# Polysketch attention and a wave MLP on one core: zero matmuls in TensorE's early gaps, and the work of GpSimd given to VectorE

## Chip, core and metric

The kernel runs on one core of one Trainium2 chip. The metric is device time in microseconds (us): before the change 283.65 us, the median of three runs (283.55 to 283.65). The profiled execution has a span of 282.6 us from its first instruction to its last, at a mean granted TensorE clock of 0.962. Engines: PE is TensorE (PEld its weight loads), DVE VectorE, ACT ScalarE, POOL GpSimd, SP the engine that issues the DMAs.

## What is computed

Two blocks in a row. First an attention with a sketched kernel: with `phi(x)` the 64 products of two 8-wide projections of x,

```python
a = einsum('rd,bhsd->bhsr', S1, x); b = einsum('rd,bhsd->bhsr', S2, x)
phi = einsum('bhsi,bhsj->bhsij', a, b).reshape(..., 64)
kv, z = einsum('bhsf,bhsd->bhfd', phi(k), v), phi(k).sum(axis=2)
attn = einsum(phi(q), kv) / (einsum(phi(q), z) + 1e-6)     # 4 batches, 4 heads, 1088 tokens, 32
```

Then, with x the attention output as 4 batches of 1088 x 128:

```python
theta = x @ w_theta
y = einsum('ts,bsd->btd', w_tok_r, x * cos(theta)) + einsum('ts,bsd->btd', w_tok_i, x * sin(theta))
u = x + y
out = u + maximum(u @ w_ch, 0)
```

The weights come as 64-bit floats and are unpacked on the chip. The denominator of the attention can come close to zero, so the sums behind it are kept in several slices of lower precision that are exact in themselves; this is most of the small work of the first third.

## The kernel before

The 1088 tokens are nine chunks of 128 (the last is half full), handled in three groups of three chunks. A batch goes through these stages.

- **Key sums** (`key_sums`). ACT squares k for a scale; DVE rounds k to a bf16 slice, subtracts it, rounds the remainder to a second slice (1152 columns each). PE multiplies the slices with themselves (18 bf16 matmuls of 128x256 and 128x128). What is left, the "rest of k", is another subtraction: for batch 0 on DVE in three pieces of 384, for batches 1 to 3 on POOL in three pieces of 384; then a 1152-column scalar_tensor_tensor on DVE and nine fp32 matmuls.
- **Key features** (`kfeatures`). PE transposes k, ACT copies it, PE multiplies by the block matrix `sbk` (128x64 for each chunk), ACT copies the 192 columns of a group from PSUM into `ks`, and POOL forms the outer products in pieces of 256 columns: 3 pieces x 3 groups x 4 batches = 36. PE then sums them with v. The pieces wait for `gate`, which a POOL copy writes after the chain of batch 0.
- **Chain** (`chain`): some 25 small DVE operations and a few small matmuls which turn the key sums into the last columns of the query matrices `mv` and `mf`. Batch 0 has a chain of its own; batches 1, 2 and 3 share one.
- **Query** (`query_slices`, `levels`, `outputs_x`): q is transposed, scaled, sliced, multiplied by `mv` and `mf` (the "levels", 36 matmuls for each batch), the denominator is worked out on DVE in `lv`, and outer products of `lv` are formed, on DVE for batch 0 (three operations of 768 columns) and on POOL for batches 1 to 3 (27 pieces of 256). They are transposed, multiplied with kv, and then theta, sine and cosine give `z`, the moving side of the mixing (`zs<-ps,g`, 768 columns, once for each full group).
- **Mixing** (`mix_row`): 17 rows of token weights (128 x 1088, fp32) for each batch, three matmuls each: 204 matmuls, the bulk of PE's work. A row must be unpacked first (`weight`): three activations on ACT (L610, L612, L614) and two operations on DVE (a shift of 1088 columns, L360, and an integer add, shown as CUSTOM_DVE_ANT_0 of 2176 uint16).
- **Output** (`mix_out`): add, multiply by w_ch, relu, add, DMA out.

The order of all this is not the order of the text. Every operation is registered with an engine, a cost and its buffers (`op`, `vop`); `Layout.run` works a due time back from the end, adds a shift for the operation's stage from the table `SHIFT`, and `forward` lays out one order for each engine by due time, cost and free buffers. Then `issue` writes the instructions in that order. On the chip every engine takes its instructions strictly in that order. So costs, shifts and the choice of engine all move the order; the hardware's own timing does not.

Line numbers in the profile are those of the kernel before. Most operations go through helpers: L356 is every tensor_tensor, L360 every tensor_scalar, L363 every scalar_tensor_tensor, L372 every plain matmul, so groups are told apart by their tiles.

Of the kernel before, what the change touches and what calls it, by code (L numbers as in the profile page):

```python
# [22 lines left out]
P = 128  # L23
# [11 lines left out]
    "blocks_k": -115.0, "blocks_m": -165.9, "blocks_t": 172.5, "chain0": -493.9, "chain1": -25.2, "den0": -154.1,  # L35
    "den1": -0.6, "den2": 550.3, "den3": 155.9, "first": -13.6, "gate": 68.2, "grid0": -47.2, "grid1": -361.7,
    "grid2": -154.8, "grid3": 138.2, "kT0": -616.5, "kT1": -15.8, "kT2": -106.5, "kT3": 114.8, "keys0": 58.1,
    "keys1": -64.3, "keys2": -6.4, "keys3": 9.8, "kf0": -371.9, "kf1": 82.0, "kf2": -122.3, "kf3": -269.6,
    "kv0": 177.9, "kv1": -3.1, "kv2": -165.7, "kv3": -145.7, "kvb0": -73.2, "kvb1": 78.1, "levels0": 27.7,
    "levels1": -326.9, "levels2": 9.3, "levels3": 197.7, "loadk0": -211.2, "loadk1": 67.3, "loadk2": -116.1,  # L40
    "loadk3": 80.6, "loadq0": -176.1, "loadq1": -113.3, "loadq2": 36.5, "loadq3": 71.0, "loadv0": -5.3,
    "loadv1": -52.2, "loadv2": -248.7, "loadv3": -299.6, "mix0_0": 129.2, "mix1_0": 202.6, "mix1_1": 115.4,
    "mix1_2": 151.5, "mix2_0": 347.7, "mix2_1": 356.4, "mix2_2": 310.8, "mix3_0": -119.0, "mix3_1": -118.6,
    "mix3_2": 366.5, "num0_0": -225.0, "num0_1": -212.0, "num0_2": -155.2, "num1_0": -203.1, "num1_1": -151.6,
    "num1_2": -192.6, "num2_0": -37.1, "num2_1": -88.4, "num2_2": 110.9, "num3_0": 55.3, "num3_1": 19.1,
    "num3_2": -106.3, "out0_0": -36.1, "out0_1": 126.0, "out0_2": 20.0, "out1_0": 347.1, "out1_1": 95.9,
    "out1_2": 143.3, "out2_0": 709.5, "out2_1": 7.1, "out2_2": -127.5, "out3_0": 347.1, "out3_1": -81.0,
    "out3_2": 475.1, "q00": 131.5, "q01": 143.4, "q02": 329.5, "q03": 362.9, "qT0": -50.6, "qT1": -265.7,
    "qT2": -56.8, "qT3": 76.7, "qscale0": 126.6, "qscale1": -94.7, "qscale2": -43.4, "qscale3": 44.4, "rest0": -58.6,
    "rest1": -254.4, "rest2": -245.4, "rest3": -265.7, "row0": -150.0, "row1": 39.7, "row10": 44.3, "row11": 49.1,  # L50
    "row12": 50.4, "row13": 49.7, "row14": 50.7, "row15": 56.2, "row16": -107.5, "row2": 27.1, "row3": 5.8,
    "row4": -56.8, "row5": 44.6, "row6": 40.1, "row7": -5.9, "row8": -184.9, "row9": 39.3, "scaled": -96.4,
    "sliced": 94.2, "small": -110.5, "square2": -101.4, "sums0": 317.9, "sums1": 343.8, "sums2": 425.5,
    "sums3": 183.2, "theta0_0": -278.2, "theta0_1": -308.1, "theta0_2": 44.1, "theta1_0": -213.8, "theta1_1": -58.7,
    "theta1_2": -139.2, "theta2_0": 183.5, "theta2_1": 199.8, "theta2_2": 168.6, "theta3_0": -54.6,
    "theta3_1": 142.0, "theta3_2": 139.8, "w2": -16.1,
}
LOAD_LEAD = 60.0
RAW_LEAD = 30.0
CHAINS = ((0,), (1, 2, 3))  # L60
QPOOL = (False, True, True, True)
# [19 lines left out]
class Layout:  # L81


    START = {"P": 1.3, "V": 0.8, "A": 0.7, "G": 1.3, "S": 0.5}
    ISSUE = 0.4
# [71 lines left out]
    def forward(self):  # L157
# [21 lines left out]
        def place(o):  # L179
            t = 0.0  # L180
            need = {}
            for b in o.bufs:
                if b.slot is None and b.cls is not None:
                    need.setdefault(b.cls, []).append(b)
            for c, bs in need.items():
                av = sorted(s[0] for s in slots[c] if s[1] is None)
                last = max((b.due, b.ops[0]) for b in bs)
                before = bisect.bisect_left(pending[c], last, key=lambda x: x[:2]) - len(bs) + 1
                if len(av) < len(bs) + min(max(before, 0), self.RESERVE[c]):
                    return None  # L190
                t = max(t, av[len(bs) - 1])
            return t

        while done < len(ops):
            pick = None
            for e in "PVAGS":
                cand = []
                for o in ready[e]:
                    t = max(free[e], o.ready, o.due - o.lead)
                    p = place(o)  # L200
                    if p is None:
                        continue
                    t = max(t, p)
                    if o.lk:
                        a, z, n = port["V" if e == "G" else "G"]
                        if a <= t < z:
                            t = z if n == 1 else min(z, t + 0.25)
                    cand.append((t, o))
                if not cand:
                    continue  # L210
                first = min(c[0] for c in cand)
                t, o = min((c for c in cand if c[0] <= first + self.SLACK[e]), key=lambda c: (c[1].rank, c[1].i))
                if pick is None or t < pick[0]:
                    pick = (t, o)
            if pick is None:
                raise RuntimeError("no room: " + str([(o.eng, round(o.due), [b.name for b in o.bufs]) for e in "PVAGS"
                                                      for o in ready[e]]))
# [38 lines left out]
    def issue(self, pools):  # L256
        for o in self.order:
            for b in o.bufs:
                if b.ap is None:
                    b.ap = view(pools[b.cls](b.slot), b.shape, b.dt)  # L260
            o.fn()
# [33 lines left out]
def kernel(  # L295
# [107 lines left out]
    op("V", 1.0, constants, [hm, bdm, halfpi, steps, ups, ones], [])  # L403
    op("A", 1.6, lambda: A.activation(warm(), halfpi(), AF.Sin), [warm], [halfpi], due=0.0)
# [13 lines left out]
    if wide:  # L418
# [4 lines left out]
        op("A", 0.4 * H + 0.4, read_small, [st], [], due=-9.0, fly=2.0)  # L423
# [86 lines left out]
    op("G", 1.3, sliced, [cm, c16, cf], [sc, sf], lk=7)  # L510
# [24 lines left out]
    op("G", 0.5, blocks_k, [s32, sbk], [sp, hm], lk=2)  # L535
# [40 lines left out]
    op("G", 0.9, spread2, [sx2, psc], [s0, sc], lk=4)  # L576
# [26 lines left out]
    def weight(dst, dfn, src, n, due=None):  # L603
# [8 lines left out]
        op("A", 0.24 + n * 0.00105, lambda: A.activation(stp()[:, :, 1].bitcast(F16), words_of(raw(), n)[1].bitcast(F32),  # L612
                                                     AF.Copy, scale=2.0**-60), [(stp, 1)], [raw])
        op("A", 0.24 + n * 0.00105, lambda: A.activation(stp()[:, :, 0], words_of(raw(), n)[0].bitcast(U32), AF.Copy,  # L614
# [3 lines left out]
        op("V", n * 0.0012 + 0.08, lambda: tt(V, dfn().bitcast(I32), dfn().bitcast(I32),  # L618
# [16 lines left out]
    def key_sums(b):  # L635
# [25 lines left out]
        op("V", 0.3, key_steps, [(km, 0)], [(km, 1), steps], lk=1)  # L661
# [11 lines left out]
        for c in range(NC):  # L673
            op("P", 0.22, lambda c=c: levels_of(c), [(t, "l")], [kb])
        at("rest", b)
        kh = buf("big", (NC, HD), F32, "kh")
        for g in range(NG):
            x = slice(g * GC, (g + 1) * GC)
            if b == 0:
                vop(GW, lambda x=x: tt(V, r()[:, x], r()[:, x], kb()[:, 1, x], ALU.subtract), [(r, g)], [(kb, 1)], lk=1)  # L680
                vop(GW, lambda x=x: stt(kh()[:, x], r()[:, x], -0.5, kx()[:, x].rearrange("p c h d -> p c (h d)"),
                                        ALU.mult, ALU.add), [(kh, g)], [(r, g), kx], lk=1)
            else:
                op("G", 0.93, lambda x=x: tt(G, r()[:, x], r()[:, x], kb()[:, 1, x], ALU.subtract), [(r, g)],
                   [(kb, 1), gate], lk=1)
# [15 lines left out]
    def kfeatures(b):  # L701
# [3 lines left out]
        for g in range(NG):  # L705
# [3 lines left out]
            ks = buf("sm", (CH, 2 * R), F32, "ks")  # L709
# [17 lines left out]
            op("A", act(CH * 2 * R), lambda kf=kf, ks=ks: A.copy(ks().rearrange("p n r -> p (n r)"), kf()), [ks], [kf])  # L727

            at("kv", b)

            def outer(i, kp=kp, ks=ks):
                h = slice(i * H, (i + 1) * H)
                tt(G, kp()[:, h], bc(ks()[:, h, 0:R], 3, [P, H, R, R]), bc(ks()[:, h, R:2 * R], 2, [P, H, R, R]), ALU.mult)

            for i in range(GC):
                op("G", 0.64, lambda i=i, f=outer: f(i), [(kp, i)], [ks, gate], lk=1)
# [20 lines left out]
    def chain(bs):  # L757
# [3 lines left out]
        for b in bs:  # L761
# [10 lines left out]
            op("V", 1.25, split, [e0, e1], [t, kg[b], kg[b, 0]], lk=1)  # L772
# [135 lines left out]
    def levels(b):  # L908
# [43 lines left out]
        op("V", 0.75, finish_den, [dn], [(ep[b], 1)], lk=2)  # L952
# [5 lines left out]
    def outputs_x(b, lv, pool_qp):  # L958
# [3 lines left out]
        for g in range(NG):  # L962
# [54 lines left out]
            op("A", act(GW) + .08, lambda cs=cs: A.activation(cs()[:, 0], cs()[:, 0], AF.Sin, bias=halfpi(),  # L1017
                                                              scale=-TWO_PI), [(cs, 0)], [halfpi])
            op("A", act(GW) + .08, lambda cs=cs: A.activation(cs()[:, 1], cs()[:, 1], AF.Sin, scale=-TWO_PI), [(cs, 1)],  # L1019
# [77 lines left out]
    for bs in CHAINS:  # L1097
# [6 lines left out]
        if not bs[0]:  # L1104
            at("gate")
            op("G", 0.1, lambda nu=nus[bs]: G.tensor_copy(gate(), nu()[:, 0, 0:1]), [gate], [nus[bs]], lk=1)
            for b in bs:
                kfeatures(b)
        chain_out(bs)
    for b in range(B):  # L1110
        query_slices(b)
# [20 lines left out]
    with tc.manual_schedule():  # L1132
        L.issue(pools)
# [43 lines left out]
```

## Time and profile before

| engine | busy us | share of the span | instructions |
|---|---|---|---|
| PE | 253.1 | 90% | 1447 |
| PEld | 187.9 | 67% | 1447 |
| DVE | 162.2 | 57% | 337 |
| ACT | 142.8 | 51% | 231 |
| POOL | 77.4 | 27% | 112 |

The share of an engine is a mean over stages with different limits, so the span has to be read in stretches: the early part, where k and q are prepared, and the part where the mixing runs. The row of the granted clock says how fast PE was allowed to run in each stretch. POOL's 77.4 us are 36 outer products of k (35.6 us), 27 of q (20.4 us), nine pieces of the rest of k (11.1 us) and small copies. Some matmul ends are modelled, so a busy PE is not PE at its peak.

### The profile page before, as it was taken

The numbers are of one execution on the slowest core, as the hardware profiler recorded it, in microseconds if no ns is written. First come the engines' busy times: TensorE is split into PE (matmuls) and PEld (weight loads), VectorE is DVE, ScalarE is ACT, GpSimd is POOL, SyncE is SP. The second block draws the span as 40 slices with busy tenths as digits, with TensorE's granted clock in tenths as the row PEclk, the third lists the DMA queues.
The fourth block names the chain that finished last, engine by engine and source line by source line (L and its number), as shares of the span: only waits on it lengthen the run. The fifth ranks groups of instructions, "written<-read, shape, count | busy, mean of one in ns | idle before, by whom it ended". The sixth has DMA issues, their size and how long they took to land.

```text
span 282.6 us, 3841 instructions
## 1 busy us (share of the span) xinstructions
PE 253.1 (90%) x1447; PEld 187.9 (67%) x1447; DVE 162.2 (57%) x337; ACT 142.8 (51%) x231; POOL 77.4 (27%) x112
## 2 busy tenths in 40 slices
PE   3596898588599899997999999999999999999993
PEld 3495797467497767664776687657876755565762
DVE  1768769999799999899564078104652400010102
ACT  4569953367667898977898040334606700000101
POOL 0291024999954800085000000700042000000000
PEclk9999557999989999999999999999999999999999
DMA  7999924406404018441500012000000000010011
GB/s 260 388 420 422 409 84 159 160 0 247 154 0 160 1 16 302 143 175 44 198 2 0 0 52 58 0 23 0 2 28 23 2 0 0 0 30 0 1 54 52
DMA packets 9154, 28.77 MB, mean 102 GB/s; under 512 B 944, under 2 KB 5296, under 8 KB 6960
## 3 DMA queue, kind: packets, MB, share of 16 engines
q1 hardware_dynamic: 8928, 28.51, 27.2%
q8 instruction: 11, 0.18, 0.3%
q14 instruction: 7, 0.06, 0.1%
q10 hardware_dynamic: 208, 0.02, 0.1%
HBM read 26.30 MB, written 2.23 MB: 101 GB/s over the span
## 4 chain that ended last, share of the span: by engine, by line
PE 61%; DVE 16%; POOL 9%; ACT 7%; issue 3%; DMA 2%; SPq 0%; DVEq 0%; ACTq 0%
PE ps L372 56%; POOL g L356 5%; DVE big L356 4%; POOL big L356 3%; DVE big L360 2%; DMA big<-q_l 2%; ACT big L614 2%; ACT big L612 2%; DVE lv L356 2%; PE ps L982 2%; DVE sm L356 2%; PE ps L1070 1%; DVE big L363 1%; ACT big L610 1%; PE ps L1004 1%
## 5 line engine op out<-in xcount | busy, mean ns | idle before, releaser
L372 PE MATMUL ps<-big,zs 128*128 128x384 f32 (+1 forms) x408 | 128.6, 469 | 0.0
L372 PEld LDWEIGHTS ps<-big,zs 128*128 128x128 f32 x408 | 75.6, 190 | 42.7 <-issue 0.8
L356 POOL TENSOR_TENSOR g<-lv 128x256 f32<-128x256 f32 x27 | 20.4, 790 | 95.9 <-DVE lv L356 95.9
L1080 ACT ACTIVATE g<-ps 128x384 f32<-128x384 f32 (+2 forms) x16 | 6.2, 406 | 65.8 <-PE ps L372 65.8
L356 POOL TENSOR_TENSOR g<-sm 128x256 f32<-128x256 f32 x36 | 35.6, 1024 | 6.7 <-ACT sm L727 6.7
L356 DVE TENSOR_TENSOR g<-big,ps 128x384 f32<-128x384 f32 (+1 forms) x12 | 6.4, 530 | 52.5 <-PE ps L372 52.5
L356 DVE CUSTOM_DVE_ANT_0 big<-big,big 128x2176 uint16<-128x2176 uint16 x17 | 23.9, 1404 | 5.1 <-ACT big L614 4.6
L612 ACT ACTIVATE big<-zs 128x1088 f16<-128x1088 f32 (+1 forms) x18 | 24.8, 1380 | 0.0
L614 ACT ACTIVATE big<-zs 128x1088 int16<-128x1088 uint32 (+1 forms) x18 | 24.8, 1376 | 0.0
L986 ACT COPY g<-ps 128x384 f32<-128x384 f32 x24 | 10.3, 483 | 22.3 <-PE ps L982 20.6
L610 ACT ACTIVATE big<-zs 128x1088 f32<-128x1088 f32 x17 | 20.5, 1213 | 0.6 <-DMA zs<-w_tok 0.6
L372 PE MATMUL ps<-big,big 128*128 128x128 f32 x72 | 11.4, 318 | 7.9 <-DVE big L363 7.8
L372 PEld LDWEIGHTS ps<-big,big 128*128 128x128 f32 x72 | 10.1, 222 | 9.0 <-DVE big L363 9.0
L356 DVE TENSOR_TENSOR zs<-ps,g 128x768 f32<-128x768 f32 (+2 forms) x20 | 12.0, 630 | 6.2 <-ACT g L1019 6.1
L360 DVE TENSOR_SCALAR big<-big 128x1088 int32<-128x1088 int32 x17 | 14.8, 869 | 1.1 <-ACT big L610 1.1
L363 DVE SCALAR_TENSOR_TENSOR g<-g,ps 128x384 f32<-128x384 f32 x12 | 6.6, 552 | 14.8 <-ACT g L1013 14.8
L356 DVE TENSOR_TENSOR g<-g,ps 128x384 f32<-128x384 f32 (+2 forms) x16 | 6.9, 450 | 14.0 <-ACT g L1080 9.0
L372 PE MATMUL ps<-mf,big 128*128 128x96 f32 x72 | 14.4, 295 | 0.5 <-DVE big L356 0.5
L372 PE MATMUL ps<-sbk,g 128*128 128x64 f32 x72 | 13.9, 359 | 0.8 <-POOL sbk L356 0.8
L372 PEld LDWEIGHTS ps<-sbk,g 128*128 128x128 f32 x72 | 13.1, 273 | 1.3 <-POOL sbk L356 0.9
L372 PE MATMUL ps<-g,big 128*64 128x128 f32 x144 | 11.4, 293 | 2.5 <-POOL g L356 2.5
L714 PE MATMUL ps<-ident,big 128*128 128x128 f32 x36 | 8.1, 389 | 4.8 <-DMA big<-k_l 4.8
(163 smaller groups left out, 391.8 us busy)
## 6 DMA issues: line engine op xcount, KB each, us to landing
zs<-w_tok SPq DMA_DIRECT2D x17, 1088.0 KB, 6.1
big<-k_l SPq DMA_DIRECT2D x4, 576.0 KB, 10.0
big<-v_l SPq DMA_DIRECT2D x4, 576.0 KB, 6.3
big<-q_l SPq DMA_DIRECT2D x4, 576.0 KB, 5.2
out<-g SPq DMA_DIRECT2D x8, 192.0 KB, 2.1
out<-g SPq DMA_DIRECT2D x4, 128.0 KB, 1.8
zs<-w_sq SPq DMA_DIRECT2D x1, 256.0 KB, 14.3
out<-g SPq DMA_DIRECT2D x4, 32.0 KB, 1.8
```

The lines of the kernel that those rows point to most:

```text
L356: eng.tensor_tensor(out=o, in0=a, in1=b, op=f)
L360: (eng or V).tensor_scalar(out=o, in0=a, scalar1=s1, scalar2=s2, op0=op0, **kw)
L363: (eng or V).scalar_tensor_tensor(out=o, in0=a, scalar=s, in1=b, op0=op0, op1=op1)
L372: T.matmul(o, lhs, rhs, start=start, stop=stop, skip_group_check=True)
L610: op("A", 0.22 + n * 0.0009, lambda: A.activation(dfn(), words_of(raw(), n)[1].bitcast(F32), AF.Copy, scale=2.0**-112), [dst], [raw])
L612: op("A", 0.24 + n * 0.00105, lambda: A.activation(stp()[:, :, 1].bitcast(F16), words_of(raw(), n)[1].bitcast(F32), AF.Copy, scale=2.0**-6 ...
L614: op("A", 0.24 + n * 0.00105, lambda: A.activation(stp()[:, :, 0], words_of(raw(), n)[0].bitcast(U32), AF.Copy, scale=2.0**-29), [(stp, 0) ...
L714: T.transpose(tr()[:, i * P:(i + 1) * P], kx()[:, g * GC + i].rearrange("p h d -> p (h d)"), ident())
L982: T.transpose(tr()[:, i * P:(i + 1) * P], qp()[:, i * H + 2 * n:i * H + 2 * n + 2].rearrange("p h i j -> p (h i j)"), ident())
L986: op("A", act(GW), lambda n=n, tr=tr, qT=qT: A.copy(qT()[:, n], tr()), [(qT, n)], [tr])
L1004: T.transpose(x()[:, i], y_, ident())
L1080: op("A", act(m), lambda n=n, i0=i0, i1=i1, o=o: A.activation(o(), po()[:n, i0 * P:i1 * P], AF.Relu), [(ot, j)], [po])
```

## The change

Four things, and a new order that follows from them.

- **Fillers.** A matmul of zeros, 128x384 in bf16, into a PSUM bank that nothing reads. Eleven stand at the start of PE's order. After that, `issue` puts `int((gap - 0.08) * 5)` of them ahead of each PE operation, where gap is the pause in us that the layout expects there; this ends with a last one behind the kv sum of batch 0. The bank is held until then, so seven of eight are left for other use. In the order that results there are 107 fillers.
- **No outer products and no rests of k on POOL** (`QPOOL`, `KPOOL`, `RPOOL` all False). The outer products of k become one DVE operation of 768 columns for each group (12 in all) that takes one factor straight from PSUM, so ACT copies only 96 columns to `ks`. The rest of k of batches 1 to 3 becomes one DVE operation of 1152 columns each, and the outer products of q of batches 1 to 3 become nine DVE operations of 768.
- **Shifts and costs.** Every entry of `SHIFT` is new, and some costs of the layout are changed a little.
- **The layout's search.** Engines are tried in another order, and where no operation has room for its buffers with the reserve kept, a second choice without the reserve is tried.

```diff
+WARM = 0
+FILL = 5.0
-QPOOL = (False, True, True, True)
+QPOOL = (False, False, False, False)
+KPOOL = (False, False, False, False)
+RPOOL = (False, False, False, False)
...
+        last, on = 0.0, False
         for o in self.order:
+            if o.eng == "P":
+                if on:
+                    for _ in range(int((o.start - last - 0.08) * FILL)):
+                        fill()
+                last, on = o.end, on and o is not span[1] or o is span[0]
...
+    def spin():
+        T.matmul(nowhere(), idle()[:, 0:P], idle(), start=True, stop=True, skip_group_check=True)
+
+    op("G", 0.3, lambda: G.memset(idle(), 0.0), [idle], [], due=-20.0)
+    first = op("P", 3.2, lambda: [spin() for _ in range(11)], [nowhere], [idle], due=-10.0)
...
+        if b and not RPOOL[b]:
+            vop(n, lambda: tt(V, flat(r()), flat(r()), flat(kb()[:, 1]), ALU.subtract), [r], [(kb, 1)], lk=1)
...
-            for i in range(GC):
-                op("G", 0.64, lambda i=i, f=outer: f(i), [(kp, i)], [ks, gate], lk=1)
+            if KPOOL[b]:
+                for i in range(GC):
+                    op("G", 0.64, lambda i=i, f=outer, ks=ks: f(G, slice(i * H, (i + 1) * H), ks), [(kp, i)], [ks, gate],
+                       lk=1)
+            else:
+                vop(CH * R * R, lambda f=outer, fv=fv: f(V, slice(0, CH), fv), [kp], [ks, kf])
...
+        if not bs[0]:
+            last = op("P", 0.1, spin, [nowhere], [kvb[WARM]] if WARM < B else [idle])
```

## The prediction

> **What bounds the kernel now.** I read the table by stretches first: busy time of each engine between two moments (us, PE, PEld, DVE, ACT, POOL, granted clock, DMA share, GB/s).
>
> ```profile
> 0.00:20.00 20.00, 11.96 (x54) 11.26 (x55) 11.15 (x58) 11.01 (x20) 7.92 (x28) 1.00 0.91 353
> 20.00:30.00 10.00, 6.89 (x46) 5.72 (x44) 7.44 (x12) 9.75 (x12) 2.27 (x12) 0.95 1.02 416
> 30.00:43.00 13.00, 11.96 (x53) 11.21 (x53) 9.00 (x32) 9.39 (x14) 2.38 (x5) 0.50 0.53 216
> 43.00:70.00 27.00, 21.00 (x207) 17.99 (x206) 26.41 (x32) 13.41 (x22) 23.46 (x22) 0.94 0.40 144
> 70.00:80.00 10.00, 6.63 (x53) 6.09 (x52) 8.44 (x11) 5.07 (x7) 10.00 (x11) 0.84 0.33 120
> 80.00:102.97 22.97, 21.28 (x209) 17.86 (x208) 22.45 (x43) 19.51 (x37) 10.98 (x11) 0.99 0.14 50
> 102.97:135.00 32.03, 30.13 (x151) 20.13 (x151) 30.01 (x65) 27.29 (x32) 9.76 (x9) 1.00 0.46 159
> 135.00:277.79 142.79, 142.79 (x690) 97.48 (x686) 46.71 (x88) 46.78 (x90) 10.61 (x18) 1.00 0.07 21
> ```
>
> The first mixing matmul starts at 102.97. From there to 277.79 PE is busy 172.9 of 174.8 us at full clock: nothing but less PE work or an earlier start shortens that part. Before 102.97 PE is not full, while DVE is (26.41 of 27 us from 43 to 70). So the question is when mixing can start. The chain of waits says what holds it (start, length, what):
>
> ```profile
> 47.27 5.60 POOL big L356 x5
> ...
> 58.45 13.20 POOL g L356 x13
> 71.65 2.71 POOL big L356 x3
> 74.38 1.77 DVE big L363
> ...
> 97.14 1.81 DVE zs L356 x2
> ```
>
> From 47 to 74 POOL's outer products and rests of k carry the chain, then DVE, until z of batch 0 is written at 98.95. The groups of DVE instructions, first in the stretch 47 to 77 where POOL is busy, then in 0 to 47:
>
> ```profile
> L363 DVE SCALAR_TENSOR_TENSOR big<-big,big 128x1152 f32<-128x1152 f32 x3 | 5.6, 1869 | 1.4 <-POOL big L356 1.4
> L360 DVE TENSOR_SCALAR big<-big,sm 128x1152 bf16<-128x1152 f32 x4 | 4.4, 1090 | 0.1
> L356 DVE CUSTOM_DVE_ANT_0 big<-big,big 128x2176 uint16<-128x2176 uint16 x2 | 3.5, 1748 | 0.1
> ```
> ```profile
> L360 DVE TENSOR_SCALAR big<-big,sm 128x1152 bf16<-128x1152 f32 x5 | 4.4, 873 | 0.0
> L356 DVE TENSOR_TENSOR big<-big,big 128x1152 f32<-128x1152 f32 x3 | 4.1, 1351 | 0.1
> L356 DVE CUSTOM_DVE_ANT_0 big<-big,big 128x2176 uint16<-128x2176 uint16 x3 | 3.9, 1285 | 0.6 <-ACT big L614 0.6
> ```
>
> The same shapes take 25 to 36% longer beside POOL. To 98.95 DVE is busy 81.1 us and idle 17.8.
>
> **What the skill says.** The Trainium skill, "SBUF — State Buffer", section "SBUF: two separate sides", says that DVE (with two SBUF inputs or in a two-port mode) and GpSimd share a port pair by an exclusive lock, the loser waiting; the 1285 against 1748 ns agree in direction. "VectorE: DVE Perf Modes", section "Why PSUM operands drop a tier", says that an fp32 operand in PSUM means one element per cycle; the trace has 952 ns for 768 columns from PSUM (zs<-ps,g) and 953 ns for 768 from SBUF (g<-lv), so PSUM costs an outer product nothing more. "TensorE: Matmul & The Clock Gate", section "Part 1: The HAM clock gate (the "warmup" mystery)", says that an idle PE falls to half clock and needs a few us of sustained work to get back. The trace agrees with 0.50 from 30 to 43; for 0 to 20 it records 1.00, yet 18 transposes take 2.18 us at 8.1 and 1.20 at 84.0, so I read half speed there too.
>
> **The change part by part.**
>
> *POOL to DVE.* Twelve outer products of k at 0.95 us = 11.4 us and three rests of k at 1.35 = 4.05 go onto DVE ahead of mixing. They replace 36 pieces on POOL (mean 1024 ns, 35.6 us busy) and nine (1266 ns, 11.1). I summed DVE's issue order, with undisturbed durations, up to the write of z that the first mixing matmul needs (164 rows now, 153 before). Before: 70.4 us. After: plus 15.5 for these, plus 2.1 (one more batch of query slices first), plus 1.6 (the shared chain of batches 1 to 3 is now finished first); minus what now comes later: five row adds (5 x 1.28), six row shifts (6 x 0.72), one z (0.95), one 384-column operation (0.55), together 12.2. That is 77.3. Neighbouring DVE operations overlap a little: where POOL is quiet (100 to 135), my durations add to 31.1 us and the trace needs 29.8 once its 1.7 of waits and about 2.7 of slowed operations are taken off. So I scale by 0.955: 67.2 before, against 81.1 measured (13.9 of contention), and 73.8 after with no contention left but POOL's small copies.
>
> *DVE's waits.* At least 7.3 us: k arrives at 4.75 and ACT's square takes 1.3; then the first outer product cannot start until sbk (POOL), the first row activation queued ahead of the `ks` copy on ACT, and that row's transfer (ninth in SP's queue, behind eight of 0.59 MB: 5.8 MB at the 353 GB/s of the first 20 us, some 17 us, and up to 2 more for what is in flight beside it) are through, near 20.3 us, while only 13.0 us of DVE work stand ahead. Further waits come from PE and ACT in their fixed orders. Following the three orders by hand to the first z I find 1 to 2 us more; before had 17.8 in all. I take 11.5, from 7.3 to 18. First mixing: 73.8 + 11.5 + 0.2 = 85.5, from 81.3 to 92.
>
> *Fillers.* 107. The bf16 key sums run 18 instructions of 192 columns on average in 1.66 us, about 0.08 each, so 384 columns take 0.16: 17 us of PE, or 34 at half clock. Before mixing PE is busy 79.7 us now; halving the 24 us at half speed leaves about 67. 67 - 3.6 + 17 = 81 of 85 us: they fit, hidden behind DVE, but barely. A filler cannot be skipped when its gap is shorter than laid out; what queues behind it is a real matmul, and DVE or ACT wait for that. I cost this inside the 11.5. What they save is half-clock PE work of 12 us, which mostly waits for DVE anyway: worth nothing by itself, but it keeps PE's answers short.
>
> *Mixing part.* PE's order has, behind the first mixing matmul, the same 204 mixing matmuls and 27 levels groups, plus 18 transposes (0.11 each, L1004 takes 0.33 for three), two of 64x384 (0.36), three theta matmuls (0.22) and one with ones (0.2): 3.6 us. So 172.9 + 3.6 = 176.5.
>
> *Rows.* Only three rows are unpacked at that moment against eight before; DVE needs 51.8 x 0.955 = 49.5 us more to unpack the last. Following PE's order, it stands about 3.7 us in the first 28 (row 4, outer products of batch 1, first z of batch 1), then has more than enough mixing of batches 0 and 1. With 1.3 for later waits I take 5 (3 to 12), against 1.9 before. The nine outer products of q (8.6 us on DVE) lie behind mixing: from 135 on DVE is busy 46.7 of 142.8 us.
>
> *ACT* saves 12 x about 0.08 us; hidden, since it doesn't set the start. The end keeps 5.85 us (283.65 - 277.8), plus 0.3 since the last output is a full group.
>
> Sum: 85.5 + 176.5 + 5.0 + 6.15 = 273.15, say 273.
>
> **Rivals.**
> - *Smooth start* (0.20): DVE waits only what the first data force. 81.3 + 176.5 + 3 + 6.15 = 267. For: DVE was 98% busy from 43 to 70. Against: a whole new order with PE nearly full.
> - *Fillers in the way* (0.15): gaps shorter than laid out or a cold clock, PE late by some 8 us. 93.5 + 176.5 + 5 + 6.15 = 281.
> - *DVE becomes the bound* (0.15, slower): as many waits as before (73.8 + 18 + 0.2 = 92) and rows too late, since 14 of 17 are still packed: 12 us of PE standing. 92 + 176.5 + 12 + 6.15 = 286.7. For: DVE and ACT both carry some 46 to 50 us in those 50 us, so a slip on either delays rows.
> - The likeliest, 273, has 0.47; 0.03 is left for no difference, between the last two.
>
> **Numbers.** Range 265 to 284: it takes in the smooth start, the likeliest case and the fillers, and leaves out most of the slower one. Faster 0.82, same 0.03, slower 0.15.
>
> **What would show it.** Right: first mixing matmul at 81 to 92; row adds near 1.28 and 1152-column operations near 1.35 us throughout; DVE busy about 74 us up to the first z; outer products of k at 0.95; clock 1.00 from some 7 us on; PE standing 3 to 12 us behind the start of mixing. Wrong: DVE idle over 18 us ahead of mixing, waits of DVE or ACT on PE with fillers ahead of the matmul waited for, or long waits of mixing for row adds.

## The result, and the profile after

The kernel with the change takes 271.23 us (median of 4 runs, 270.61 to 273.26) against 283.6 us beside it: 0.958 of the time, with a 95% interval of 0.953 to 0.964. Most of the kernels below scatter by some us from run to run, the longer times going with the lower mean granted clocks (the kernel after: 270.96 us at 1.000, 273.26 at 0.986); where that matters I give the range.

First the table by stretches (columns as before: stretch, us, then busy time of PE, PEld, DVE, ACT and POOL with the number of instructions, granted clock, DMA share, GB/s):

```profile
0.00:20.00 20.00, 17.11 (x106) 11.13 (x107) 12.40 (x62) 11.92 (x23) 3.23 (x18) 1.00 0.92 354
20.00:30.00 10.00, 9.54 (x107) 8.57 (x107) 9.52 (x18) 7.15 (x15) 4.90 (x23) 1.00 0.98 380
30.00:43.00 13.00, 13.00 (x133) 12.01 (x128) 11.45 (x30) 7.65 (x14) 0.00 (x0) 1.00 0.62 242
...
0.00:84.19 84.19, 77.62 (x686) 62.62 (x686) 73.10 (x181) 62.06 (x99) 8.31 (x41) 1.00 0.63 233
...
85.04:117.00 31.96, 29.87 (x174) 20.27 (x174) 29.69 (x67) 22.61 (x38) 0.00 (x0) 1.00 0.10 36
117.00:264.53 147.53, 147.53 (x692) 100.15 (x691) 62.61 (x111) 56.45 (x94) 0.00 (x0) 1.00 0.14 52
```

84.19 is where the first z that mixing needs has been written, and 85.04 where the first mixing matmul starts: 17.9 us earlier than the 102.97 of before. Up to the z DVE is busy 73.1 us and idle 11.1. PE is busy 77.6 of these 84.2 us, now at a recorded clock of 1.00 throughout (0.50 from 30 to 43 before). Behind the start of mixing PE is busy 29.87 + 147.53 = 177.4 us and stands 2.1. So the whole gain lies ahead of mixing, and 4.5 us of it is given back behind, where 177.4 us of PE work stand against 172.9.

The chain of waits of the kernel after, in pieces (start, length, what):

```profile
8.92 9.44 DMA zs<-w_tok
18.38 1.08 ACT big L632
19.73 0.96 DVE g L370
...
24.04 15.10 PE ps L386 x154
...
45.19 1.46 PE ps L421 x9
...
69.06 1.37 DVE big L370
...
83.47 0.99 PE ps L386 x6
```

POOL, which carried it from 47 to 74 us before, is gone from it: a transfer of the first row, its first activation on ACT, the first outer product of k, then PE up to 57.1 us, and from there almost only DVE. From 20.74 to 57.14 PE is busy without a break (36.40 of 36.40 us; DVE 33.89), so in this stretch PE sets the pace as much as DVE does. L421 are fillers: four short groups of them, 2.6 us in all, are on the chain, so not all fillers are hidden. The groups of DVE instructions with their shapes, from 0 to 84.19:

```profile
L370 DVE TENSOR_TENSOR g<-sm,ps 128x768 f32<-128x768 f32 x12 | 11.0, 948 | 0.6 <-ACT sm L752 0.6
L370 DVE TENSOR_TENSOR big<-big,big 128x1152 f32<-128x1152 f32 x7 | 9.5, 1354 | 0.1
L370 DVE CUSTOM_DVE_ANT_0 big<-big,big 128x2176 uint16<-128x2176 uint16 x3 | 3.9, 1289 | 0.1
L377 DVE SCALAR_TENSOR_TENSOR big<-big,big 128x1152 f32<-128x1152 f32 x3 | 4.1, 1358 | 0.1
```

The twelve outer products of k are here at 948 ns, and the shapes that took 1748 and 1869 ns beside POOL are at 1289 and 1358. That is why DVE's busy time over the whole program grew by only 4.6 us (162.2 to 166.9), although operations worth 24 us of its time came to it from POOL (12 x 0.95, 3 x 1.35 and 9 x 0.95).

### The profile page after: what moved, and what is told of

Its sections match the earlier page's. It is cut to its first block, busy times and chain, and to the rows that moved or that the text cites. A ratio compares the mean times of both kernels' runs of the same rounds, so it can differ in the third digit from the quotient of the medians.

```text
span 269.2 us, 3987 instructions
## 1 busy us (share of the span) xinstructions
PE 256.1 (95%) x1554; PEld 183.8 (68%) x1554; DVE 166.9 (62%) x361; ACT 141.6 (53%) x231; POOL 8.3 (3%) x41
## 4 chain that ended last, share of the span: by engine, by line
PE 74%; DVE 15%; DMA 6%; issue 2%; ACT 1%; SPq 0%; ACTq 0%
PE ps L386 66%; DMA zs<-w_tok 4%; DVE g L370 3%; PE ps L1011 3%; DVE lv L370 2%; DMA st<-s_t 2%; DVE sm L370 2%; DVE big L370 2%; PE ps L1099 2%; DVE big L374 1%; PE ps L927 1%; PE ps L1033 1%; DVE big L377 1%; PE ps L738 1%; PE ps L421 1%
## 5 line engine op out<-in xcount | busy, mean ns | idle before, releaser
L421 PE MATMUL ps<-idle 128*128 128x384 bf16 x107 | 20.8, 342 | 1.3 <-POOL idle L423 1.3
L421 PEld LDWEIGHTS <-idle 128*128 128x128 bf16 x107 | 10.8, 105 | 7.7 <-issue 1.5
L930 ACT ACTIVATE big<-ps,qs 128x384 f32<-128x384 f32 x12 | 6.5, 585 | 16.4 <-PE ps L927 16.4
L1011 PE MATMUL ps<-ident,g 128*128 128x128 f32 x72 | 10.6, 277 | 1.7 <-DVE g L370 1.7
L374 DVE TENSOR_SCALAR big<-big 128x1088 int32<-128x1088 int32 x17 | 12.1, 719 | 0.0
L1011 PEld LDWEIGHTS ps<-ident,g 128*128 128x128 f32 x72 | 8.1, 141 | 5.3 <-issue 2.9
L370 DVE TENSOR_TENSOR g<-sm,ps 128x768 f32<-128x768 f32 x12 | 11.0, 948 | 0.6 <-ACT sm L752 0.6
L370 DVE TENSOR_TENSOR g<-lv 128x768 f32<-128x768 f32 x12 | 11.2, 950 | 0.1
L386 PEld LDWEIGHTS ps<-w,big 128*128 128x128 f32 x72 | 9.3, 192 | 2.9 <-ACT big L1024 1.4
L370 DVE TENSOR_TENSOR big<-big,big 128x1152 f32<-128x1152 f32 (+1 forms) x10 | 11.1, 1114 | 0.1
## 6 DMA issues: line engine op xcount, KB each, us to landing
zs<-w_sq SPq DMA_DIRECT2D x1, 256.0 KB, 12.2
```

Of the source, the lines that this page charges most:

```text
L370: eng.tensor_tensor(out=o, in0=a, in1=b, op=f)
L374: (eng or V).tensor_scalar(out=o, in0=a, scalar1=s1, scalar2=s2, op0=op0, **kw)
L386: T.matmul(o, lhs, rhs, start=start, stop=stop, skip_group_check=True)
L421: T.matmul(nowhere(), idle()[:, 0:P], idle(), start=True, stop=True, skip_group_check=True)
L930: op("A", act(GW) + 0.1, lambda g=g, tr=tr: A.activation(f()[:, g * GW:(g + 1) * GW], tr(), AF.Copy, scale=s()[:, 0:1]), [(f, g)], [tr, (s ...
L1011: T.transpose(tr()[:, i * P:(i + 1) * P], qp()[:, i * H + 2 * n:i * H + 2 * n + 2].rearrange("p h i j -> p (h i j)"), ident())
```

## The experiments

**Theory**, as the prediction has it: taking work off POOL makes the gain, since it ends DVE's slow-down and takes POOL out of the chain; fillers only keep PE's answers short and are worth nothing by themselves. **Rivals**: the fillers make the gain (R1), or the new order of the work makes it (R2). To keep order and engine apart, each kernel below leaves the order of one of the two kernels as it is and changes only what is told.

### The kernel after without its fillers

```diff
-FILL = 5.0
+FILL = 0.0
-    first = op("P", 3.2, lambda: [spin() for _ in range(11)], [nowhere], [idle], due=-10.0)
+    first = op("P", 3.2, lambda: [spin() for _ in range(1)], [nowhere], [idle], due=-10.0)
```

> The kernel after, in its own order, with 1 filler matmul instead of 107. Theory (taking work off POOL makes the gain; the fillers only keep PE's answers short): the granted clock falls in the stretches where PE idles, PE's real work ahead of mixing takes up to 12 us longer but mostly lies beside DVE, the first mixing matmul comes 0 to 4 us later than 85.0, and the time is 271 to 275 us. Rival R1 (the fillers make most of the gain): 277 us or more, with DVE waiting 6 us or more longer on PE. Rival R2 (the new order alone makes it): 271 to 272.

Measured: 277.36 us (275.82 to 278.67), 0.976 of before (0.971 to 0.982). That is 6.1 us more than with fillers, half of the gain. DVE has the same order in both kernels, so its timelines can be laid side by side. With fillers:

```profile
23.05 1.19 DVE L374 TENSOR_SCALAR big<-big,sm 128x1152 bf16<-128x1152 f32 x1
24.19 0.16 DVE L374 TENSOR_SCALAR sm<-ps 128x1 f32<-128x1 f32 x1
...
83.24 0.95 DVE L370 TENSOR_TENSOR zs<-ps,g 128x768 f32<-128x768 f32 x1
84.49 0.26 DVE L838 TENSOR_REDUCE sm<-ps 128x12 f32<-128x96 f32 x1 [0.30 <-PE ps L386]
```

The same operations without fillers:

```profile
23.87 0.92 DVE L374 TENSOR_SCALAR big<-big,sm 128x1152 bf16<-128x1152 f32 x1
27.91 0.16 DVE L374 TENSOR_SCALAR sm<-ps 128x1 f32<-128x1 f32 x1 [3.13 <-PE ps L386]
...
81.92 0.29 DVE L370 TENSOR_TENSOR sm<-ps,hf 128x128 f32<-128x128 f32 x1 [1.69 <-PE ps L386]
88.46 0.95 DVE L370 TENSOR_TENSOR zs<-ps,g 128x768 f32<-128x768 f32 x1
90.51 0.26 DVE L838 TENSOR_REDUCE sm<-ps 128x12 f32<-128x96 f32 x1 [1.10 <-PE ps L386]
```

DVE does the same work in the same time (73.3 us up to the end of the z, 73.1 with fillers); it is 3.7 us later after one wait on PE (27.91 against 24.19), 5.2 at the z, 6.0 at the reduction of L838. What it waits for is a matmul of one column, queued behind the features and sums of k. PE's timeline without fillers:

```profile
17.71 4.10 PE L386 MATMUL ps<-sbk,g 128*128 128x64 f32 x18 [3.79 <-POOL sbk L370]
24.69 2.59 PE L386 MATMUL ps<-g,big 128*64 128x128 f32 x24
27.59 0.28 PE L386 MATMUL ps<-sm,ones 128*128 128x1 f32 x2
...
69.51 1.51 PE L1011 MATMUL ps<-ident,g 128*128 128x128 f32 x6 [4.82 <-DVE g L370]
72.56 2.54 PE L386 MATMUL ps<-g,sm 128*64 128x384 f32 x8
```

The first group takes 4.10 us here and 2.12 in the kernel after: a cold PE. The later one is cold again after PE stood 4.8 us. The page "TensorE: Matmul & The Clock Gate" of the Trainium skill, section "HAM oscillation — how this bites in real kernels", says that idle gaps of over some 3.4 us bring the half clock back; the clock of 0.53 from 70 to 75 us here agrees. But PE also turns cold without such a gap, as the next section shows. The time is longer than the 271 to 275 us expected, and R1 is half right: the fillers are worth 6 us in this order, through DVE's waits for PE.

### Only the early, only the late fillers

```diff
-                    for _ in range(int((o.start - last - 0.08) * FILL)):
+                    for _ in range(int((o.start - last - 0.08) * FILL) if o.start < 30.0 else 0):
```

The other kernel has `> 30.0` and one filler at the start.

> The kernel after with only those 61 fillers that the layout places ahead of 30 us; the 46 later ones are left out. New theory, read from the kernel without fillers (277.4 us), where DVE falls 3.72 us behind in one wait for PE at 24.2 to 27.9 us and another 2.5 us in waits for PE at 76 to 91: the cold clock up to 26 us costs 3.7, the idle PE at 61 to 70 costs 2.5. So the wait at 24 is gone, those at 76 to 91 stay: 273 to 274.5 us. Rival (only an unbroken row of fillers holds the clock; half of them are worth nothing): 276 or more. Rival (only the early ones count): 271 to 272.

> The kernel after with one filler at the start and the 46 that the layout places behind 30 us; the 60 others are left out. New theory: the wait of 3.7 us at 24 to 28 us is there, those of 2.5 us at 76 to 91 are gone: 274 to 275.5 us. Rival (the late ones count alone): 271 to 272. Rival (half of them are worth nothing): 276 or more.

Measured: early ones only, 272.74 to 280.32 us with a median of 276.35, the two shorter runs 0.968 of before (0.961 to 0.975); late ones only, 273.74 to 277.30 with a median of 276.12, 0.973 (0.968 to 0.979). Both medians lie above what was expected, and where the rival has them that half of the fillers are worth nothing; both intervals overlap that of the kernel without fillers (0.971 to 0.982), and the first also that of the kernel with all. So the times alone do not divide the 6 us. The traces do, in part. With the late ones only, DVE falls 2.7 us behind at the wait at 24 us and nothing more up to the z, and the first mixing matmul is at 87.73: the late fillers do take the later waits away. With the early ones only, DVE loses 1.8 us in the wait near 76 and 0.6 near 85, as expected; but it had lost 1.9 already at 24, although PE's order up to there is that of the kernel after. PE's timeline with the early fillers only:

```profile
12.03 0.59 PE L386 MATMUL ps<-sm,ones 128*128 128x1 f32 x2 [1.44 <-ACT big L666]
...
13.79 1.89 PE L421 MATMUL ps<-idle 128*128 128x384 bf16 x6
```

A transfer of k came 0.8 us later than in the trace of the kernel after (ACT goes on with it at 10.72 us instead of 9.91). PE stood 1.44 us, and the next six fillers ran at half speed (1.89 us against 1.14) and stood in the way of what followed. So fillers don't keep PE warm in every run, and here no gap came near 3.4 us.

The same order of work can also come out warm in one run and cold in another. Mixing starts in the kernel after with the first of these lines, and with the second in the kernel below that has the outer products of q on POOL:

```profile
85.04 5.73 PE L386 MATMUL ps<-big,zs 128*128 128x384 f32 x18
85.30 7.42 PE L386 MATMUL ps<-big,zs 128*128 128x384 f32 x18
```

Ahead of both, PE has the same fillers, does the same work and stands 1.4 and 0.35 us; yet the first is granted 1.00 and the second 0.77 over the 7.4 us. The skill's same page says, in "What's actually happening", that the clock's window is not tied to the kernel's start; these two traces would fit that, but no run here tests it. In the traces, mixing starts cold in every kernel of the new order but two, the kernel after and the one with the late fillers: its first 18 matmuls take 7.1 to 8.4 us instead of 5.73. The times below contain this.

### More fillers than the gaps hold

```diff
-FILL = 5.0
+FILL = 8.0
```

> The kernel after with fillers laid out at 8 instead of 5 for each us of gap: 168 instead of 107, each some 0.16 us, so more than the gaps hold. Theory (PE was busy 77.6 of the first 84.2 us, a filler can't be skipped, and DVE waits in order for the matmul behind it): 61 x 0.16 = 10 us more PE work into 6.6 us of room, first mixing 3 to 8 us later, 274 to 279 us. Rival (PE has room enough, or a steadier clock pays for it): 270 to 272.

Measured: 277.90 us, 0.982 of before (0.978 to 0.987): 6.7 us more than with 107. The first mixing matmul is at 91.10. Up to there PE is busy 87.0 of 91.1 us, and DVE's losses are waits again: 2.7 us behind at the first outer product, 3.1 at 24, 4.5 at 59, 6.0 at 77. The two shortest runs, 277.35 and 277.39, have mean clocks of 0.999 and 1.000, so this loss needs no cold PE. Too few fillers and too many cost the same, by the same way: DVE waits in order for a matmul that comes late. Fewer than 107 spread over the whole early part were not tried.

### The outer products and rests back on POOL, all and one kind at a time

In the order of the kernel after, with its fillers. The edits, which are all in the first of these kernels, and one by one in the other three (with the outer products of k, ACT also copies all 192 columns to `ks` again):

```diff
-                vop(CH * R * R, lambda f=outer, fv=fv: f(V, slice(0, CH), fv), [kp], [ks, kf])
+                vop(CH * R * R, lambda f=outer, ks=ks: [f(G, slice(i * H, (i + 1) * H), ks) for i in range(GC)], [kp], [ks, kf])
...
-            vop(n, lambda: tt(V, flat(r()), flat(r()), flat(kb()[:, 1]), ALU.subtract), [r], [(kb, 1)], lk=1)
+            vop(n, lambda: [tt(G, r()[:, x], r()[:, x], kb()[:, 1, x], ALU.subtract)
+                            for x in (slice(g * GC, (g + 1) * GC) for g in range(NG))], [r], [(kb, 1)], lk=1)
...
-                vop(CH * R * R, lambda f=outer: f(V, 0, 1), [qp], [lv], lk=1)
+                vop(CH * R * R, lambda f=outer: [f(G, i, GC) for i in range(GC)] if b else f(V, 0, 1), [qp], [lv], lk=1)
```

> The kernel after, in its own order and with its fillers; only the engine of 36 pieces of outer products of k, 9 pieces of rests of k and 27 pieces of outer products of q of batches 1 to 3 is POOL again, as before. Theory: POOL carries 36 x 1.02 + 9 x 1.27 = some 48 us ahead of mixing again, DVE's 1152-column operations are 25 to 36% longer beside it although DVE has 15 us less to do, and the first mixing matmul comes 10 us or more later: 281 to 290 us. Rivals R1 (fillers) and R2 (order): fillers and order are unchanged, so the time stays within 3 us of 271.2.

> The kernel after, in its own order and with its fillers, with only the 12 outer products of k on POOL again (36 pieces of 256 columns). The rests alone gave 276.5 us, all three kinds 293.1. Theory (in this order DVE's work has been put straight behind each outer product, so each trio of pieces, 2.5 to 3 us on POOL against 0.95 on DVE, is waited for through PE's sums): first mixing 7 to 13 us later, 279 to 285 us. Rival (the rests and what piles up behind them are the main cost): 272 to 276.

> The kernel after, in its own order and with its fillers, with only the 3 rests of k (as 9 pieces of 384 columns) on POOL again. With all three kinds back (293.1 us) DVE waited 16.1 us in 3 waits for the rests. Theory (in this order the rest of k stands straight ahead of DVE's next operation, which waits for POOL's 3 pieces): three times some 2.7 us on POOL in place of 1.35 on DVE, 1.4 + 0.3 each, 4 to 6 us in all: 274 to 278 us. Rival (the outer products of k ahead of them in POOL's queue made those 16 us): within 1.5 us of 271.2 if the POOL pieces are hidden, since nothing is queued ahead of them now.

> The kernel after, in its own order and with its fillers, with only the 9 outer products of q of batches 1 to 3 on POOL again (27 pieces of 256 columns). Prediction: they lie behind the start of mixing, where DVE has time; first mixing unchanged at 85, and PE has mixing of batch 0 to do meanwhile: within 1 us of 271.2. Rival (batch 1's come at 101 to 105, where PE has little mixing in reserve, and take 2.5 to 3 us each instead of 0.95): PE stands 3 to 5 us longer, 274 to 276.

| back on POOL | us | of before | first mixing matmul at |
|---|---|---|---|
| nothing (the kernel after) | 271.23 | 0.958 (0.953 to 0.964) | 85.04 |
| outer products of k | 286.20 | 1.009 (1.006 to 1.012) | 98.14 |
| rests of k | 276.54 | 0.977 (0.972 to 0.981) | 88.67 |
| outer products of q, batches 1 to 3 | 279.27 | 0.986 (0.982 to 0.990) | 85.30 |
| all three | 293.08 | 1.031 (1.027 to 1.034) | 96.91 |

One by one they cost 15.0, 5.3 and 8.0 us, together 21.9. All three came out 2 us longer than the 281 to 290 expected and the outer products of k 1 us longer than their 285; the rests lie inside; for the outer products of q the expectation was wrong, and its rival's 276 too short as well. New order and fillers with POOL at its old work are slower than before: R2 falls as an explanation of its own. Since this order was made for DVE, 21.9 us is what undoing the move costs in it, not the price of POOL in an order of POOL's own. DVE's waits up to the z, with all three back:

```profile
DVE big L377 <- POOL big L370: 16.1, 3, 8.4
DVE sm L374 <- PE ps L386: 7.3, 1, 7.3
```

and with only the rests of k back:

```profile
DVE big L377 <- POOL big L370: 7.6, 3, 2.9
```

Three times POOL's pieces are waited for straight away. With only the rests back this is 7.6 us of waits against 4.05 of DVE work saved: 3.5, and the first mixing matmul is 3.6 us later. The total of 5.3 has in it that mixing starts cold in that trace. With the outer products of k alone, DVE waits 16.5 us on PE up to the z (0.8 with none back), and PE in its turn waits for POOL: its matmuls 5.3 us in five waits, its weight loads 9.2 in twelve (36 pieces, 869 ns each).

The outer products of q were a surprise. Mixing starts on time, and yet 8 us are lost. Some 1.5 us of them are not POOL's doing: mixing starts cold in this trace (the 7.42 us above), and DVE ends the work ahead of the first of these products at 103.1 instead of 101.6. PE's timeline behind that, with the outer products of q on POOL:

```profile
103.96 0.33 PE L1011 MATMUL ps<-ident,g 128*128 128x128 f32 x1
104.54 0.33 PE L1011 MATMUL ps<-ident,g 128*128 128x128 f32 x1 [0.25 <-POOL g L370]
...
107.90 0.33 PE L1011 MATMUL ps<-ident,g 128*128 128x128 f32 x1 [1.31 <-POOL g L370]
...
112.17 1.34 PE L386 MATMUL ps<-g,sm 128*64 128x384 f32 x4
...
116.09 1.99 PE L386 MATMUL ps<-big,zs 128*128 128x384 f32 x6
```

Nine pieces take POOL from 103.28 to 111.71 where DVE needs 2.8 us for the three whole products. PE's order has no mixing between 100.7 and 116.09; it stands 4.3 us in six waits for POOL here and once at 187, turns cold (1.34 us for four matmuls that take 0.87 in the kernel after), and the six mixing matmuls at 116.09 are those that start at 109.14 there. "Behind the start of mixing" was not yet "hidden".

### Contention alone

The kernel after, with work on POOL that nothing waits for:

```diff
-            op("G", 0.1, lambda: G.tensor_copy(gate(), mf[0]()[:, 2, 0, 0:1]), [gate], [(mf[0], "y")], lk=1)
+            def gated():
+                G.tensor_copy(gate(), mf[0]()[:, 2, 0, 0:1])
+                for _ in range(30):
+                    tt(G, junk()[:, 1], junk()[:, 0], junk()[:, 0], ALU.mult)
+
+            op("G", 0.1, gated, [gate], [(mf[0], "y")], lk=1)
```

> The kernel after, and in addition 30 multiplications of 256 columns of a scratch tile on POOL from about 54 us on, for which nothing waits. Theory (contention is a cost of its own): beside them DVE's operations with operands in SBUF take 25 to 36% longer as in the kernel before (1152-column adds 1.35 to some 1.8 us, row adds 1.29 to 1.75), over some 25 us, and the first mixing matmul comes 4 to 8 us later: 275 to 280 us. Rival (what POOL's work cost before was only that others waited for it): 271 to 272.

Measured: 281.11 us, 0.990 of before (0.985 to 0.995), so 9.9 us more than without. Groups of DVE instructions in the kernel after, 54 to 78 us:

```profile
L370 DVE TENSOR_TENSOR g<-sm,ps 128x768 f32<-128x768 f32 x3 | 2.8, 945 | 0.0
L370 DVE TENSOR_TENSOR big<-big,big 128x1152 f32<-128x1152 f32 x2 | 2.7, 1354 | 0.0
L374 DVE TENSOR_SCALAR big<-big 128x1088 int32<-128x1088 int32 x3 | 2.2, 719 | 0.0
L370 DVE TENSOR_TENSOR g<-lv 128x768 f32<-128x768 f32 x2 | 1.9, 952 | 0.0
```

The same operations with POOL's idle work beside them, 54 to 85 us:

```profile
L370 DVE TENSOR_TENSOR big<-big,big 128x1152 f32<-128x1152 f32 x2 | 3.4, 1707 | 0.0
L374 DVE TENSOR_SCALAR big<-big 128x1088 int32<-128x1088 int32 x3 | 3.4, 1131 | 0.0
L370 DVE TENSOR_TENSOR g<-lv 128x768 f32<-128x768 f32 x2 | 2.4, 1205 | 0.0
L370 DVE TENSOR_TENSOR g<-sm,ps 128x768 f32<-128x768 f32 x2 | 1.8, 940 | 0.0
```

The expected 275 to 280 us are missed by 1; the direction is the theory's. 28.2 us of POOL work that nobody needs make DVE 7.84 us later at the operation that starts at 76.72 in the kernel after; 0.48 of that was there before POOL's work began, so it costs 7.4, with hardly a wait in between. The rest comes behind it, as PE, standing more often, turns cold (clock 0.82 from 70 to 85): DVE waits 1.1 us for it near 93, and the first 18 mixing matmuls take 8.40 us. The section "SBUF: two separate sides" of "SBUF — State Buffer" says that one of the two engines holds the ports for its whole instruction and the other waits. Sign and victims agree in the groups shown (the product with an operand in PSUM is untouched); in size these operations grow by 0.25 to 0.41 us each, a quarter to under a half of one POOL piece (0.94).

### DVE instead of POOL in the order of before

```diff
-                tt(G, kp()[:, h], bc(ks()[:, h, 0:R], 3, [P, H, R, R]), bc(ks()[:, h, R:2 * R], 2, [P, H, R, R]), ALU.mult)
+                if i == 0:
+                    tt(V, kp(), bc(ks()[:, :, 0:R], 3, [P, CH, R, R]), bc(ks()[:, :, R:2 * R], 2, [P, CH, R, R]), ALU.mult)
```

The rests of k and the outer products of q of batches 1 to 3 are moved in the same way.

> The kernel before, in its own order and without fillers; only the engine of the same outer products and rests is DVE (12 + 9 outer products of 768 columns, 3 rests of 1152, whole, at the place of their first piece). Theory: contention is gone (1152-column adds at 1.35 us throughout), POOL leaves the chain, and DVE has 67.2 + 14.8 = 82 us ahead of mixing instead of 81.1 with contention; the gain is in waits, 17.8 to some 11 to 14: first mixing 93 to 97, time 275 to 279. R1 and R2: no fillers and the old order, so 283 or more.

Measured: 283.61 us, 1.000 of before (0.998 to 1.002). The theory falls as it stood: the move alone is worth nothing. Its first half came true: up to the end of z DVE is busy 78.5 us instead of 81.1, although ten outer products and three rests, 13.6 us, have come to it, so that some 16 us of contention are gone by this estimate. The chain of waits of this kernel shows where the gain stays:

```profile
93.52 1.82 DVE zs L356 x2
95.34 0.88 DVE g L356
96.26 2.76 PE ps L372 x24
99.02 1.19 PE ps L982 x6
100.21 0.66 PE ps L898 x6
100.87 2.69 PE ps L372 x18
103.89 10.29 PE ps L372 x61
```

z of batch 0 starts at 93.52, 3.6 us earlier than before. But an outer product of k of a later batch stands behind it in DVE's queue, its sums stand ahead of mixing in PE's order, and some 7.6 us of PE work follow, 1.2 of them because PE is cold after a wait of 3.1 us (24 matmuls in 2.76 us, which take 1.53 warm): mixing starts at 103.87, where it had been 102.97. In an order made for POOL, the product arrives when the z does.

### Fillers in the order of before, without and with that move

No bank is free in this order, so each filler is written to the bank that the next real matmul overwrites, ahead of operations that are first on a fresh bank:

```diff
+                if on and fresh is not None:
+                    for _ in range(int((o.start - last - 0.08) * FILL)):
+                        fill(fresh)
```

> The kernel before, in its own order and with POOL at its work, plus 126 filler matmuls of 384 columns of zeros in PE's gaps as the layout foresees them, each into the bank that the next real matmul overwrites. Theory: the granted clock rises in 30 to 43 us (0.50 before) but POOL and DVE still set the start of mixing: first mixing 101 to 103, time 282 to 284. Rival R1 (fillers make most of the gain): 271 to 277. R2: 283 to 284.

> The kernel before in its own order, with both other parts of the change: all outer products and rests of k whole on DVE, and 126 fillers. Without the fillers this gave 283.6 us: z of batch 0 was written 3.6 us earlier than before, but the last outer product of batch 3 stood behind it in DVE's queue, and its sums ahead of the first mixing matmul in PE's. Theory (that order is what keeps the gain back): the outer product still ends near 96, PE has 7.6 us of work behind it, first mixing at 101 to 104, 281 to 284 us. Rival (only the clock, 0.50 from 30 to 43 and 0.66 from 70 to 80, kept it back): first mixing near 96, 275 to 278.

The trace of each of the two has 63 fillers, not the 126 announced. Measured: with POOL at its work, 16 of 20 runs between 284.0 and 286.5 us and four between 279.7 and 281.4 (these four 0.989 of before, 0.987 to 0.992); with the move as well, 284.5, 286.5, 286.6 and 279.8. Most runs are up to 3 us longer than expected, and none comes to the 271 to 277 of R1. Both have been traced near 284 only. With POOL at its work, the stretch from 30 to 43 us reads

```profile
30.00:43.00 13.00, 13.00 (x59) 10.81 (x59) 7.84 (x31) 7.93 (x14) 2.50 (x6) 0.52 0.50 205
```

18 fillers stand in this stretch and PE is busy in all of it, and yet the clock is 0.52 (0.51 in the other kernel, with 16). It is back at 1.00 from 43 us on, behind nine fillers in an unbroken row. So a full PE is not yet a warm one, and what holds the clock down there is open. Mixing starts at 102.84 and 104.03. In the second, PE waits 3.3 us for the same outer product behind z and has its work ahead of mixing still to do, as the theory of the order has it. So fillers and move together, without the new order, mostly give nothing. What the faster runs have that these traces lack is open, and so is what a warm PE would give in this order.

## Why the prediction was right

The sum predicted was 85.5 + 176.5 + 5.0 + 6.15; measured it is 85.04 + 177.4 + 2.1 + 6.43 (4.67 from the last PE work of mixing to the end of the span, 1.76 from there to the time of that run, 270.96).

- **DVE's work up to the first z**: predicted 73.8, measured 73.1. Contention of 13.9 us gone was the step with most in it, and it is shown from both sides: durations are the undisturbed ones throughout, the move in the old order takes some 16 us of it away, and putting useless work on POOL brings 7.4 us back within some 30. The sum also had the new order in it, as the 12.2 us of DVE work that now come later, but gave it no weight of its own.
- **Its waits**: predicted 11.5 (7.3 to 18), measured 11.1. The first outer product starts at 19.73 (predicted 20.3), held by the first row's transfer and activation, as foreseen; 7.6 us of the waits stand ahead of it (predicted 7.3). Behind it 3.5 us were measured, where 1 to 2 had been found by hand and the rest was a margin: so close a hit is partly luck.
- **PE's work behind the start of mixing**: predicted 176.5, measured 177.4.
- **PE standing** behind it: predicted 5, measured 2.1. This is the term of the sum that was mis-sized. Rows and z came in time; there are three waits of 0.6 to 0.8 us.
- **Fillers**: 20.8 us of PE instead of 17, but at the start-to-start time assumed (25 in 4.22 us). They fit "barely", as said: 77.6 of 84.2 us, and from 20.7 to 57.1 not quite hidden, since PE has no pause left there. **What failed is the step "worth nothing by itself"**: without them, the waits of DVE ahead of the z are 16.1 us (89.4 less 73.3) instead of 11.1, and the time is 6.1 us longer. It was argued that half-clock PE work mostly waits for DVE anyway; but DVE waits for PE in a few places, in order (3.1 us at 24, 1.7 at 80), and there a late answer costs in full. The result held because the 11.5 us were taken with a PE that answers fast.
- **Two readings of the trace**: the view has nine transposes at 8.1 and at 84.0, not 18; 2.18 against 1.20 us still tells a cold start. And 0.50 from 30 to 43 was called agreement with the page's idle PE; but PE is busy 11.96 of those 13.00 us, and the kernel of before with fillers, busy in all 13.00, has 0.52. So the half clock was there, but not for the reason given.
- **q behind mixing, hidden**: true of DVE, where PE waited 0.8 us for these products once. As a general step it was wrong: on POOL they cost some 6.5 of the 8 us, with mixing already started.
- **The rivals**: "Fillers in the way" is real, and begins not far above the number chosen (168 instead of 107 give 277.9). "DVE becomes the bound" did not come: DVE is busy 29.7 of the 32 us behind the start of mixing, but PE waits for it only 1.4 us there.
- **The cause**: the prediction put the gain down to POOL. The runs show three parts that need each other. The move in the old order gives 0; move and new order 6.2 us (283.6 to 277.4); these and the fillers 12.4. Fillers and this order, made for DVE, lose 9 without the move. Move and fillers in the old order mostly give nothing, but PE was not warm in the runs of it that were traced. Which of the new costs, shifts and choices of the layout make the good order was not tried apart.

## What to carry to other kernels

Taking work off a slow engine pays only where the fixed orders of the others let the earlier result be used: look in each queue at what stands between the earlier result and its user. Fillers pay where an in-order engine waits for the answer of a cold PE, and cost as much where they outgrow the gap, so price them by the waits of the engine that sets the pace and not by PE's own time. "Behind the start of the bound stage" is hidden only once that stage has work in reserve.

## What the runs showed of the hardware

- Beside POOL's pieces of 256 columns, a short DVE operation can lose as many nanoseconds as a long one: one of 36 columns went from 195 to 617 ns, one of 4 columns from 229 to 676, those of 1088 columns from 719 to 1131, of 1152 columns with two SBUF operands from 1354 to 1707. Others nearby lost nothing: another of 36 columns took 197 both times, a reciprocal 378. A DVE product with one operand in PSUM lost nothing (945 and 940). POOL loses too: a piece of 256 columns takes 0.63 us where DVE is nearly idle (at 205 us, with the outer products of q on POOL) and 0.94 beside it.
- In the kernel without fillers, the recorded clock is 1.00 from 0 to 20 us, while the same 18 matmuls take 4.10 us there and 2.12 in the kernel after. The durations tell a cold start, the record does not.
- In the trace of the kernel after, the fillers go with a granted clock of 1.00 throughout. They do not ensure it: mixing started cold in other kernels with all 107, and 13.00 us of busy PE with 18 fillers among it had 0.52. A filler takes 0.16 us on a warm PE and 0.31 on a cold one, where it delays what it was to speed up.
